# Half-size expert slots without TensorE's prefetch hint for the next slot's branch

## The chip, the cores and the metric

The kernel runs on one core of one Trainium2 chip. The metric is device microseconds for one execution. A core has five engines with an instruction stream each: PE (TensorE, whose weight loads the profile lists apart as PEld), DVE, ACT, POOL and SP. PEq (or PEldq), DVEq and so on stand for an engine's sequencer, which issues its instructions, branches and semaphore instructions. SP issues nearly all of the DMAs here.

## What is computed

Three stages follow one another: attention with a learned position bias, a gated dense layer, and a layer of eight experts in which each of 1152 tokens goes to one expert. The change lies in the last one:

```python
def _moe2_ref(x, w_gate, w1, w2, capacity):
    logits = x @ w_gate                       # x: 1152 x 512, 8 experts
    expert_idx = np.argmax(logits, axis=1)
    ...                                       # softmax; gate_w is the chosen expert's share
    for i in range(N):                        # capacity = 288 tokens for an expert
        e = expert_idx[i]
        if counts[e] < capacity:
            disp[e, counts[e]] = x[i]
            ...
    h = np.maximum(np.einsum('ecd,edf->ecf', disp, w1), 0.0)   # 512 -> 1024
    y = np.einsum('ecf,efd->ecd', h, w2)                       # 1024 -> 512
    for i in range(N):
        if keep[i]:
            out[i] = gate_w[i] * y[expert_idx[i], pos[i]]
```

## The kernel before

**Slots.** How many tokens an expert gets is known on the chip alone. The kernel sorts the experts by their count and works through nine slots, `e` = 0 to 8, the fullest first. Slots 0 and 1 always run the code for a full expert (`full`). For the others there are four ladders of code, one behind the other, each with a body for every slot that it may be needed for: `full` from line 1404, `mid1` and `mid2` (65 to 128 tokens) from line 1410, `few1` and `few2` with `q` = 2 (half-size slots, up to 64 tokens) from line 1418, and the same two with `q` = 4 (quarter-size, up to 32 tokens) from line 1428. The counts sit in registers (`ns`), and nested `If`s choose: the outer one leaves a ladder when the slot is too small for it, and the inner one skips a body that an earlier ladder has already done.

**How a ladder is left.** In the half-size ladder the outer `If` of slot `e` has the label `q{e}` (line 1420, whose branches the profile gives as L1418), and the inner one the label `d{e}` (L1421). When slot `e + 1` has too few tokens, each engine takes the branch of `q{e + 1}`, goes to a small arm behind the last body of the ladder, waits there until its own semaphores have caught up with what the skipped bodies would have counted (an EVENT_SEMAPHORE row), and goes on to the next ladder. SP's arms have one such row for each of eight DMA semaphores.

**Hints.** `hint(label, ...)` (line 1081) puts one BRANCH_PREFETCH_HINT instruction, in a block of its own, into TensorE's stream (and into others that it names): the branch with that label is likely to be taken. The hints that stand ahead of the loops' branches are `big` in the last fixed slot (line 1316), `b{e + 1}` in `mid1` (line 1205), both for TensorE, DVE and ACT, and `q{e + 1}` in the half-size bodies (line 1423), for TensorE alone. The quarter-size ladder has none.

**A half-size body.** `few1` multiplies 64 rows of tokens with the expert's first matrix (`ps_sh`, L1152, 16 products of the program, 32 MATMUL rows in the trace), DVE makes `hst` from it, TensorE transposes it (L1168); `few2` transposes the next slot's rows (L1078), spreads the gate (L1019), multiplies with the second matrix (`ps_sy`, L1196), and `finish` scales on DVE (L1040) and scatters to the output from POOL (L678). A quarter-size body is the same with 32 rows. `load_next` (line 726) has SP load the weights of slot `e + 3` and the rows of slot `e + 6`.

**Places in the stream.** `align(n)` at a ladder's end (lines 1409, 1417, 1427) puts the code behind it at a fixed offset in 256 instructions. All of this lies in a manual schedule: the instructions stand in the order in which the code is written.

Of the kernel before, what the change touches and what calls it, by code (L numbers as in the profile page):

```python
# [514 lines left out]
def moe_kernel(ctx, tc, shape, qd, kd, vd, wb, geo, wg, wv, wo, g2, e1, e2, ebase, desc, tri, out, cap):  # L515
# [13 lines left out]
    NS = NE + 1  # L529
# [179 lines left out]
    def load_e(e):  # L709
        for n in range(8):  # L710
            k = e % 3
            if (k, n) not in raws:
                raws[k, n] = (raw_tile if k == 0 else praw if k == 2 and n < 4 else eraw(k))(F32)
            src = e1 if n < 4 else e2
            i = nc.sync.dma_start(raws[k, n], src[bass.ds(ids[e], 1), n % 4].rearrange("o p n -> (o p) n"))
            fetched.setdefault((k, n), []).append((e, i.ins))
# [9 lines left out]
    def load_next(e, more=True):  # L726
        if e + 3 < NS:
            with tc.If(nio[e + 3] > 0):  # L728
                load_e(e + 3)
                if more:  # L730
                    with tc.If(nio[e + 3] > P):
                        load_xr(e + 3, nc.gpsimd)
        if e < NS - 6:
            load_xd(e + 6)
# [49 lines left out]
    with ExitStack() as pools:  # L784
# [35 lines left out]
        def route_a(tg, parts=1):  # L820
            yt = tp.tile([P, DM], F32, tag="dt", name="yt")
            for h in range(parts):
                ps = rtile("ps_yt")
                for kc in range(h * KC // parts, (h + 1) * KC // parts):
                    nc.tensor.transpose(ps[:, kc * P:(kc + 1) * P], y[:, tg, kc * P:(kc + 1) * P], ident)
                c = slice(h * DM // parts, (h + 1) * DM // parts)
                nc.scalar.copy(yt[:, c], ps[:, c])
            rt[tg] = yt

        def route_b(tg):  # L830
            yt = rt.pop(tg)
            ps = rtile("ps_lt")
            for kc in range(KC):
                nc.tensor.matmul(
                    ps[kc * GC:(kc + 1) * GC, :P], g2_sb[:, kc], yt[:, kc * P:(kc + 1) * P],
                    start=True, stop=True, skip_group_check=True,
                )
            lt = tp.tile([P, P], F32, tag="sg", name="lt")
            nc.scalar.copy(lt, ps[:, :P])
            rt[tg] = lt  # L840

        def route_l(tg):
            lt = rt.pop(tg)
            lg = rtile("ps_r")[:, :NE]
            nc.tensor.matmul(lg, lt, sel, start=True, stop=True)
            sc = tp.tile([P, 4, NE], F32, tag="rsc", name="rsc")
            s1 = tp.tile([P, 4], F32, tag="rs1", name="rs1")
            mx, m2, nmx = (s1[:, i:i + 1] for i in range(3))
            oh = ohs[:, tg]
            nc.vector.reduce_max(mx, lg, axis=mybir.AxisListType.X)  # L850
            nc.vector.scalar_tensor_tensor(sc[:, 1], lg, mx, desc_sb, ALU.is_ge, ALU.mult)
            nc.vector.reduce_max(m2, sc[:, 1], axis=mybir.AxisListType.X)
            nc.vector.tensor_scalar(oh, desc_sb, m2, None, ALU.is_equal)
            nc.vector.tensor_scalar_mul(nmx, mx, -1.0)
            nc.vector.tensor_tensor(cum[:, tg + 1], cum[:, tg], oh, ALU.add)
            dot(sc[:, 3], ebase_sb, oh, reb[:, tg:tg + 1])
            rt[tg] = lg, nmx, sc

        def route_gate(tg):
            lg, nmx, sc = rt.pop(tg)  # L860
            nc.scalar.activation(sc[:, 2], lg, AF.Exp, bias=nmx, accum_out=rsm[:, tg:tg + 1])
# [6 lines left out]
        def route_pos(t0, t1):  # L868
            n = (t1 - t0) * NE
            pos = rtile("ps_p")[:, :n]  # L870
            nc.tensor.matmul(
                pos, tri_sb[:, :P], ohs[:, t0:t1].rearrange("p t e -> p (t e)"), start=True, stop=False
            )
            nc.tensor.matmul(pos, ones, cum[:, t0:t1].rearrange("p t e -> p (t e)"), start=False, stop=True)
            rt[t0, t1] = pos

        def route_c(t0, t1):
            pos = rt.pop((t0, t1))
            r = slice(t0, t1)
            for tg in range(t0, t1):  # L880
                sc = tp.tile([P, 4, NE], F32, tag="rsc", name="rsc")
                dot(sc[:, 0], pos[:, (tg - t0) * NE:(tg - t0 + 1) * NE], ohs[:, tg], rps[:, tg:tg + 1])
            nc.vector.tensor_scalar(rsl[:, r], rps[:, r], float(cap), BIG, ALU.is_ge, ALU.mult)
            nc.vector.tensor_scalar_add(rsm[:, r], rsm[:, r], 1e-9)
            if t1 - t0 == 1:
                nc.vector.scalar_tensor_tensor(rsi[:, r], rps[:, r], reb[:, r], rsl[:, r], ALU.add, ALU.add)
            else:
                nc.vector.tensor_tensor(rps[:, r], rps[:, r], reb[:, r], ALU.add)
                nc.vector.tensor_tensor(rsi[:, r], rps[:, r], rsl[:, r], ALU.add)
            nc.vector.reciprocal(y[:, r, DM:DM + 1], rsm[:, r].unsqueeze(2))  # L890
            for tg in range(t0, t1):
                scatter(disp[:, :], rsi[:, tg:tg + 1], y[:, tg, :], disp_w)
# [173 lines left out]
    def load_xr(e, q):  # L1066
        read_rows(q.dma_start(xr[e][:, 0, :], rows(e, P, P)))
        read_rows(q.dma_start(xr[e][:cr - P, 1, :], rows(e, 2 * P, cr - P)))
# [12 lines left out]
    def hint(label, *more):  # L1081
        with tc.block():
            tc.mark_branch_hint_location(label, hint="LikelyTaken", engines=[mybir.EngineType.PE, *more])

    def align(n):
        for eng, a in ((e, a) for e, a in ALIGN.items() if n < len(a)):
            getattr(nc, eng).addr_align(a[0], offset=a[n], max_nops=0)
# [10 lines left out]
    def wsplit(e, n):  # L1098
        for i in split(*pair(e, n), weights(e)[n].rearrange("p a n -> p (a n)")):
            own(i, e, n)  # L1100
# [281 lines left out]
    with tc.manual_schedule():  # L1382
        full(0, {
            0: [
                lambda: route_pos(T - 2, T - 1), lambda: route_c(T - 2, T - 1), lambda: route_a(T),
                lambda: route_l(T - 1), lambda: route_gate(T - 1), lambda: wsplit(0, 1),
            ],
            1: [
                lambda: route_b(T), lambda: route_pos(T - 1, T), lambda: route_c(T - 1, T),
                lambda: wsplit(0, 4),  # L1390
            ],
            2: [lambda: route_l(T), lambda: route_gate(T)],
            (2, "y"): [lambda: route_pos(T, TG), lambda: route_c(T, TG), order_experts],
            4: [begin],
        })
        load_e(2)
        with tc.If(nio[2] > P):
            load_xr(2, nc.gpsimd)
        load_next(0)
        guessed = len(out_w)  # L1400
        full(1)
        load_next(1)
        del out_w[:guessed]
        with ExitStack() as nest:
            for e in range(FIX, NS):
                nest.enter_context(tc.If(ns[e] > P, label="big" if e == FIX else f"f{e}"))
                full(e)
                load_next(e)
            align(2)
        with ExitStack() as nest:  # L1410
            for e in range(FIX, NS):
                nest.enter_context(tc.If(ns[e] > M1, label=f"b{e}"))
                with tc.If(ns[e] <= P, label=f"m{e}"):
                    mid1(e)
                    mid2(e)
                    load_next(e, False)
            align(3)
        with ExitStack() as nest:  # L1418
            for e in range(FIX, NS):
                nest.enter_context(tc.If(ns[e] > (M1 // 2 if e >= QUADS else 0), label=f"q{e}"))  # L1420
                with tc.If(ns[e] <= M1, label=f"d{e}"):  # L1421
                    if e < NS - 1:
                        hint(f"q{e + 1}")
                    few1(e, 2)
                    few2(e, 2)
                    load_next(e, False)
            align(4)
        with ExitStack() as nest:
            for e in range(QUADS, NS):
                nest.enter_context(tc.If(ns[e] > 0, label=f"z{e}"))  # L1430
                with tc.If(ns[e] <= M1 // 2, label=f"s{e}"):
                    few1(e, 4)
                    few2(e, 4)
                    load_next(e, False)
# [82 lines left out]
```

## Time and profile before

| | |
|---|---|
| runs | 508.31, 511.47, 510.93 us, median 510.93 |
| profiled execution | 511.36 us |
| its span, first to last instruction | 509.7 us |
| PE busy | 490.2 us (96%) |
| DVE, ACT, POOL busy | 370.1, 265.5, 102.1 us |
| last mid-size body on PE ends | 478.5 us from the span's start |
| half-size body on PE | 480.07 to 489.81 us |
| two quarter-size bodies on PE | 492.31 to 504.3 us |

In this execution one slot runs as mid-size, one as half-size and two as quarter-size, so the change meets one executed body. The rows ahead of the prediction are whole lines of the views. A row of an operation gives how often it ran and its shortest, median and longest time in ns; a wait names the engine that waited, for whom, and the idle microseconds, times and longest.

### The profile page before, as it was taken

To read this page: it belongs to the slowest core of one execution; us is meant where nothing else is said; L and a number is where in the kernel's file an instruction comes from. 1 tells how busy PE (TensorE), PEld (TensorE's weight loads), DVE (VectorE), ACT (ScalarE), POOL (GpSimd) and SP (SyncE) were. 2 spreads that over 40 slices of the span, in tenths; PEclk is the share of its full clock that TensorE was granted. 3 is DMA by queue.
4 is the path that set the end of the run, shared out by engine and by line. 5 is a ranking of instruction groups with operands and counts; after the bars stand their busy time and mean duration, and the time that the engine had idled before them with its cause. 6 is when DMAs were issued, how large, how long until landed. Compare 5 with 4: busy or idle time off the path is not lost. (4 is left out here: it accounts for less than half of the span.)

```text
span 509.7 us, 11908 instructions
## 1 busy us (share of the span) xinstructions
PE 490.2 (96%) x4357; PEld 405.5 (80%) x4357; DVE 370.1 (73%) x924; ACT 265.5 (52%) x604; POOL 102.1 (20%) x218
## 2 busy tenths in 40 slices
PE   7999999999999999999999999999999899999875
PEld 3467777677778999978999889999877678897554
DVE  6899999998997899996799827633356683546321
ACT  5798899998876545453544203422222534437210
POOL 1054444445551100000000000000011231702213
PEclk9999999999999999999999999999999989999989
DMA  7799789999312944353231000000013985899640
GB/s 266 262 340 336 257 272 308 314 373 290 95 50 69 323 140 139 115 182 118 80 120 50 1 1 0 2 0 1 0 43 88 395 312 167 296 407 348 234 188 11
DMA packets 50084, 89.11 MB, mean 175 GB/s; under 512 B 7970, under 2 KB 27428, under 8 KB 50000
## 3 DMA queue, kind: packets, MB, share of 16 engines
q1 hardware_dynamic: 48560, 85.04, 49.1%
q0 software_dynamic: 1296, 3.03, 1.6%
q8 instruction: 40, 0.66, 0.5%
q14 instruction: 44, 0.36, 0.2%
q10 hardware_dynamic: 144, 0.02, 0.0%
HBM read 67.00 MB, written 22.15 MB: 175 GB/s over the span
## 5 line engine op out<-in xcount | busy, mean ns | idle before, releaser
L594 PE MATMUL ps_gv<-xh,hl 128*128 128x384 f32 x528 | 135.0, 336 | 0.0
L594 PEld LDWEIGHTS ps_gv<-xh,hl 128*128 128x128 f32 x528 | 95.3, 188 | 0.1
L594 PE MATMUL ps_gv<-xl,hl 128*128 128x384 f32 x264 | 88.7, 336 | 0.0
L902 PE MATMUL ps_o<-hl,hh 128*128 128x512 f32 x216 | 73.3, 404 | 0.3 <-ACT y L907 0.3
L117 DVE TENSOR_SCALAR bt<-geo_sb 128x320 f32<-128x320 f32 (+17 forms) x144 | 58.6, 458 | 0.0
L222 ACT ACTIVATE e_sb<-e_sb,mn 128x576 f32<-128x576 f32 x72 | 56.3, 783 | 1.5 <-DVE mn L214 1.3
L235 POOL TENSOR_SCALAR e_sb<-e_sb,rs 128x576 f32<-128x576 f32 x72 | 53.3, 752 | 18.2 <-DVE rs L231 15.8
L678 POOL DMA_INDIRECT disp<-y,rsi x9 | 9.7, 1079 | 233.8 <-DVE rs L850 205.2
L214 DVE CUSTOM_DVE_ANT_0 e_sb<-ps_s,bias_sb 128x576 f32<-128x576 f32 x72 | 51.6, 751 | 2.2 <-DMA bias_sb<-bias_d 1.2
L594 PEld LDWEIGHTS ps_gv<-xl,hl 128*128 128x128 f32 x264 | 49.6, 188 | 0.1
L902 PEld LDWEIGHTS ps_o<-hl,hh 128*128 128x128 f32 x216 | 40.5, 188 | 10.5 <-issue 1.4
L300 PE MATMUL ps_x<-et,vn 128*64 128x128 f32 (+1 forms) x800 | 47.5, 267 | 0.9 <-DVE xl L318 0.8
L197 PE MATMUL ps_s<-kst,qst 64*128 64x288 f32 (+1 forms) x320 | 45.6, 423 | 0.0
L604 ACT CAST hh<-sg 128x384 fp32r<-128x384 f32 x36 | 18.4, 512 | 48.1 <-DVE sg L603 48.1
L300 PEld LDWEIGHTS ps_x<-et,vn 128*64 128x64 f32 x800 | 39.3, 137 | 4.1 <-DVE xl L318 1.5
L902 PE MATMUL ps_o<-hl,hlo 128*128 128x512 f32 x105 | 42.1, 401 | 0.0
L577 ACT CAST hl<-dg 128x512 fp32r<-128x512 f32 x32 | 19.1, 621 | 39.4 <-PE ps_o L902 21.6
L197 PEld LDWEIGHTS ps_s<-kst,qst 64*128 64x128 f32 (+1 forms) x320 | 27.0, 178 | 5.0 <-DVE mn L214 0.8
L264 PEld LDWEIGHTS ps_t<-ident,e_sb 64*128 64x128 f32 x576 | 25.2, 139 | 5.1 <-issue 0.9
L603 DVE TENSOR_TENSOR sg<-ps_gv,sg 128x384 f32<-128x384 f32 x35 | 19.3, 553 | 12.6 <-PE ps_gv L594 12.6
L1275 PE MATMUL ps_h<-dxh,hl 128*128 128x288 f32 x128 | 26.9, 301 | 0.9 <-DVE hl L565 0.9
L602 DVE TENSOR_TENSOR sg<-ps_gv,sg 128x384 f32<-128x384 f32 x35 | 19.3, 552 | 10.8 <-ACT sg L601 10.4
(237 smaller groups left out, 910.4 us busy)
## 6 DMA issues: line engine op xcount, KB each, us to landing
eraw<-e SPq DMA_DIRECT2D x24, 512.0 KB, 9.5
bias_d<-bo SPq DMA_DIRECT2D x36, 295.5 KB, 4.3
raw<-e SPq DMA_DIRECT2D x16, 512.0 KB, 10.2
raw<-wo SPq DMA_DIRECT2D x12, 512.0 KB, 4.4
raw<-wg SPq DMA_DIRECT2D x11, 512.0 KB, 3.8
raw<-wv SPq DMA_DIRECT2D x11, 512.0 KB, 5.0
disp<-zero SPq DMA_DIRECT2D x9, 520.0 KB, 4.7
bias_sb<-bias_d SPq DMA_DIRECT2D x16, 288.0 KB, 3.8
```

The lines of the kernel that those rows point to most:

```text
L117: nc.vector.tensor_scalar(t[:, :m], dist_sb[:, :m], nbp[:, r:r + 1], None, ALU.max)
L197: nc.tensor.matmul(pss[j][i, half, :HS], qst[c * B + bb][d, p, i], kst[d, bb * NP + p, half * HS:(half + 1) * HS], start=True, stop=True, ...
L214: nc.vector.tensor_tensor_reduce(out=e[:, j, :].rearrange("p (a n) -> p a n", a=2), in0=ps[:, :, :HS], in1=bias_sb[c, p][:, j, :].rearrang ...
L222: nc.scalar.activation(e[:, j, :], e[:, j, :], AF.Exp, bias=mn[:, j:j + 1], scale=-1.0, accum_out=sm[:, j:j + 1])
L235: nc.gpsimd.tensor_scalar(e[:, j, :], e[:, j, :], rs, 1.0, ALU.mult, ALU.mult)
L264: nc.tensor.transpose(tp_t[u, h][:, n * HP:(n + 1) * HP], e[r, n * P:(n + 1) * P], ident[r, r])
L300: nc.tensor.matmul(ps[j * D:(j + 1) * D, o:o + n], vn[:, p, bb, jc, j * D:(j + 1) * D], et[:, t0:t0 + n], start=jc == NF, stop=jc == NF - ...
L594: nc.tensor.matmul(ps[:, :TN], w_[:, n, kc, :], x_[:, kc, t * TN:(t + 1) * TN], start=i == 0, stop=i == 3 * KC - 1,)
L602: nc.vector.tensor_tensor(sg, pss[0][:, :TN], sg, ALU.mult)
L603: nc.vector.tensor_tensor(sg, pss[1][:, :TN], sg, ALU.mult)
L902: nc.tensor.matmul(ps, ht_cols(f, a, tg), wot[f][b_], start=i == 0, stop=i == len(ops) - 1)
L1275: nc.tensor.matmul(ps[:, :CAP], part(e, f // 2, a)[:, kc, f % 2 * P:(f % 2 + 1) * P], x_[:, kc], start=i == 0, stop=i == 3 * KC - 1,)
```

## The change

One call is left out: in a half-size body TensorE is no longer told that the branch of the next slot is likely to be taken. The hints `big` and `b{e + 1}` stay.

```diff
                 with tc.If(ns[e] <= M1, label=f"d{e}"):
-                    if e < NS - 1:
-                        hint(f"q{e + 1}")
                     few1(e, 2)
                     few2(e, 2)
                     load_next(e, False)
```

On TensorE, at the head of slot 3's half-size body (the one that runs here), the order changes as follows; `raw` holds the weights, `xt` the transposed rows.

```order
 L1418 COMPARE_AND_BRANCH
 L1421 COMPARE_AND_BRANCH
-L1082 UNCONDITIONAL_BRANCH
-L1513 BRANCH_PREFETCH_HINT
-L1082 UNCONDITIONAL_BRANCH
 L1152 MATMUL ps_sh<-raw_5234,xt_5640 64x256
 L1152 MATMUL ps_sh<-raw_5238,xt_5640 64x256
```

The hint and the two branches of its block go, and the products follow the slot's two comparisons directly. It is the same in each of six bodies (slots 2 to 7). At the end of this body nothing moves: the program's branch around the arm of line 728 and the next comparison, L1418, stay as they are.

```order
L1196 MATMUL ps_sy<-raw_5248,sht 64x256 x2
L728 UNCONDITIONAL_BRANCH
L1421 UNCONDITIONAL_BRANCH
L1418 COMPARE_AND_BRANCH
L1421 COMPARE_AND_BRANCH
L1082 UNCONDITIONAL_BRANCH
L1513 BRANCH_PREFETCH_HINT
```

These are the rows before the change, from the last products of slot 3 to the head of slot 4; the first L1418 row among them is the branch `q4`, the one that the removed hint was for. On the other engines only the block's branches go, as on DVE at a half-size body's head:

```order
 L1418 COMPARE_AND_BRANCH
 L1421 COMPARE_AND_BRANCH
-L1082 UNCONDITIONAL_BRANCH x2
 L1164 TENSOR_SCALAR hst<-ps_sh 128x256 x2
 L1173 COPY sht<-ps_st 128x256 x2
```

Every other instruction of the program, with its waits, is the same and in the same place.

## Rows read from the trace of the kernel before

**Rows 1.** The page, parts 1 and 3: engines, and the two instruction queues.
```profile
PE 490.2 (96%) x4357; PEld 405.5 (80%) x4357; DVE 370.1 (73%) x924; ACT 265.5 (52%) x604; POOL 102.1 (20%) x218
q8 instruction: 40, 0.66, 0.5%
q14 instruction: 44, 0.36, 0.2%
```
**Rows 2.** The chain that ended last, in order of time: start, us, what.
```profile
492.03 0.28 issue
492.31 2.50 PE ps_sh L1152 x32
...
502.32 2.00 PE ps_sy L1196 x64
...
504.40 0.36 DVE ob L1040
...
505.53 1.07 POOL out_dram L678
```
**Rows 3.** Timeline of PE, 470 to 511: start, us, operation [idle before <-releaser].
```profile
478.11 0.40 PE L1240 MATMUL ps_my<-hl,mhh 128*128 128x512 f32 x1
480.07 2.34 PE L1152 MATMUL ps_sh<-raw,xt 128*64 128x256 f32 x18 [1.56 <-ACTq L1421]
482.57 1.94 PE L1152 MATMUL ps_sh<-raw,xt 128*64 128x256 f32 x14 [0.16 <-issue]
...
486.14 3.67 PE L1196 MATMUL ps_sy<-raw,sht 128*64 128x256 f32 x32
492.31 2.50 PE L1152 MATMUL ps_sh<-eraw,xt 128*32 128x256 f32 x32 [2.50 <-SPq L1410]
```
**Rows 4.** Line 1513, the hints that ran: engine, count, ns, first and last start.
```profile
L1513 PEldq BRANCH_PREFETCH_HINT  x3: 36/40/41, 444.2 to 479.8; - x3
```
**Rows 5.** Line 1418, 487 to 491.5: TensorE's branch out of the half-size ladder.
```profile
L1418 PEldq COMPARE_BRANCH  x1: 3551/3551/3551, 487.8 to 487.8; - x1
L1418 PEldq EVENT_SEMAPHORE  x1: 51/51/51, 491.4 to 491.4; - x1
```
**Rows 6.** Line 1404, 462 to 464: TensorE's branch hinted as `big`.
```profile
L1404 PEldq COMPARE_BRANCH  x1: 388/388/388, 462.9 to 462.9; - x1
```
**Rows 7.** Line 1410, 476 to 478.6: TensorE's branch hinted as `b3`.
```profile
L1410 PEldq COMPARE_BRANCH  x1: 349/349/349, 476.7 to 476.7; - x1
```
**Rows 8.** Line 1428, 503 to 507: TensorE's branch without a hint.
```profile
L1428 PEldq COMPARE_BRANCH  x1: 3284/3284/3284, 503.7 to 503.7; - x1
```
**Rows 9.** DMA queues, 480 to 481.2: packets, MB, share of 16 engines.
```profile
q8 instruction: 1, 0.02, 5.0%
```
**Rows 10.** DMA queues, 481.3 to 488.8: every queue that moved anything.
```profile
DMA packets 831, 2.90 MB, mean 386 GB/s; under 512 B 118, under 2 KB 118, under 8 KB 828
q1 hardware_dynamic: 748, 2.71, 94.1%
q0 software_dynamic: 80, 0.16, 5.7%
q14 instruction: 3, 0.02, 1.0%
```
**Rows 11.** DMA queues, 488.8 to 490.
```profile
q8 instruction: 1, 0.02, 5.7%
```
**Rows 12.** Waits of PE, and SP's own, 478 to 493: us, times, longest.
```profile
PE ps_sh L1152 <- SPq L1410: 2.5, 1, 2.5
PE ps_sh L1152 <- ACTq L1421: 1.6, 1, 1.6
SPq L1410 <- SPq L1410: 9.8, 1, 9.8
```
**Rows 13.** Line 1410, 481 to 492.2: SP's arm that catches up, eight semaphores.
```profile
L1410 SPq EVENT_SEMAPHORE  x8: 17/17/17, 491.6 to 492.1; - x8
```
**Rows 14.** Weight loads of PE, waits, 478 to 493.
```profile
PEld ps_sh L1152 <- issue: 3.5, 2, 2.9
```

## The prediction

> **What bounds the kernel now.** I read the page first. PE is busy for 490.2 of 509.7 us [rows 1], so whatever PE waits for is nearly always time at the end. But the change touches PE in six bodies of which few run, so the share matters less than one place: the end of the half-size body and the step into the quarter-size ladder. Three views lead there.
>
> The chain that ended last begins at 492.03 us [rows 2]. From there PE's two quarter-size bodies run to 504.3, DVE scales the last result, POOL scatters it at 505.53, and the output's write and the closing barrier end the span. So a microsecond more or less at PE's start of 492.31 is a microsecond at the end, unless something else would hold PE back.
>
> The timeline of PE shows one half-size body: its 32 `ps_sh` rows stand at 480.07 (18) and 482.57 (14), and its last products end at 486.14 + 3.67 = 489.81 [rows 3]. Then PE idles for 2.50 us, until 492.31. This is the only idle stretch that the removed hint could concern: the profile has three hints on TensorE, and the last, at 479.8, is the one that goes [rows 4].
>
> What ends that idle time? Two things, and they end together. First, TensorE's branch at L1418, the one that the hint was for, took 3551 ns from 487.8, and its catch-up row follows at 491.4 [rows 5]. Second, the wait itself is put down to SP at L1410: SP waited 9.8 us there [rows 12], and its eight catch-up rows come only at 491.6 to 492.1 [rows 13]. The chain starts at 492.03, inside those eight, and not at the branch's end.
>
> **What the change removes, and what each piece costs.**
>
> *The hint instruction.* One of the removed hints runs in this execution, 36 ns on the sequencer [rows 4]. It stands ahead of the body's first product, but there PE idles 1.56 us until ACT's catch-up at L1421 [rows 3, 12], so those 36 ns are hidden. Without that cover they would be worth 0.04 us. The block's branches at L1082 have no row in the trace at all, on any engine, so I cost them at nothing. Five of the six removed hints lie in bodies that do not run.
>
> *What the hint buys.* Here is the heart of it. Two other hinted branches of TensorE out of a ladder took 388 and 349 ns [rows 6, 7]. One without a hint took 3284 ns [rows 8]. The branch under change has a hint and took 3551 [rows 5]: it stands with the unhinted one, not with the hinted two. A second view says the same. Queue q8 carries 40 instruction packets in 0.66 MB, about 16 KB each [rows 1]. One lands between 480 and 481.2, just after the hint [rows 9]. None at all moves between 481.3 and 488.8, while the body runs [rows 10]. The next comes between 488.8 and 490, after the branch has already begun at 487.8 [rows 11]. If the hint had brought the target in, the branch would not have had to wait for that packet. The packet at 480 must be the code of the body itself: the products stop after 18 of 32 rows and go on at 482.57 with "issue" as the reason [rows 3], as they would where the stream runs into a piece that has just come. So in this execution the hint was issued and its target was not there when it was wanted. I take its worth as zero, and the branch after the change as between 3284 and 3551 ns: 0 to 0.27 us less.
>
> The Trainium skill, "Runtime: NRT & Kernel Launch", section "Instruction fetch mechanics", says that instructions come in blocks of 16 KiB and that a taken branch whose target is outside the window must fetch it before execution goes on. The packets of 16 KB and the 3284 ns agree with that. The rule speaks against the change: by it alone a branch that loses its hint falls from a hit to a fetch, and the sum would be some 3 us longer. The row of 3551 ns is what it has to be weighed against: the fetch is paid already.
>
> *What a shorter or longer branch is worth.* Even a branch that hit would gain little. From the branch's end to the first product PE now needs 492.31 − (487.78 + 3.55) = 0.98 us. With a hit of about 0.37 us (mean of 388 and 349) PE would be ready at 487.78 + 0.37 + 0.98 = 489.13, or at 489.81 when its own products end. SP's catch-up, at 491.6 to 492.1, would then hold it to about 492.1. So here the hint's full worth is at most 492.31 − 492.03 = 0.28 us, and the 0.27 us of the last paragraph can give back no more. I take 0.1, between 0 and 0.27.
>
> *The code behind.* Each body is one instruction shorter on TensorE, so the place where the products stop after 18 rows may move by one instruction. What the stop costs is 0.16 us on PE [rows 3]; it can be 0 or that. The 3.5 us that the weight loads spend on "issue" [rows 14] are the same stop and the branch, seen from the other side of PE, and are not added. The quarter-size ladder is put at its fixed offset again by the alignment at line 1427, so nothing moves there.
>
> **Sum.** The profiled execution took 511.36 us, 509.7 of span and 1.66 around it. 511.36 + 0 (hint, hidden) − 0.1 (branch) + 0 (stop) = 511.3. Its own bounds are −0.43 (0.27 and 0.16) and +0.1. The profiled execution lies 0.43 above the median of the three runs, 510.93, and so the same sum on the median gives 510.8. The runs themselves lie between 508.31 and 511.47, 3.2 us apart, far wider than any term here; the likeliest case's own range is therefore 508.2 to 511.6.
>
> **Rivals.**
>
> *The hint usually works, and the profiled execution is the exception: slower.* The place is the same branch, L1418 at 487.8. Its price is 3.55 − 0.37 = 3.18 us if nothing else holds PE. That the three runs are 3.2 us apart, about the price of one such branch, speaks for it; so do the 388 and 349 ns of the other two hinted branches. Against it speaks that SP's catch-up at 491.6 would hold PE anyway. It decides from the point where SP is done before PE would be, that is when SP's loads land over 2 us earlier (by 489.8, the end of PE's products). Then the removal costs up to 492.31 − 489.81 = 2.5 us, or 3.18 if the products end earlier too: 513.4 to 514.1. While SP is as late as here it costs at most 0.28: 511.2. The rule of the Trainium skill named above would come out here: a lost hint is a fetch in the path.
>
> *The hint is in the way: faster.* No packet of q8 moves in the 7.5 us after the one at 480 [rows 10]. If an unserved hint blocks the ordinary fetching ahead, or delays the packet for which the products stop, its removal could save the stop and the excess of this branch over the unhinted one: 0.16 + 0.27 = 0.43 us, 510.5 on the median. SP's catch-up caps the sum at 0.28.
>
> *The change does nothing that runs.* Of the bodies that the edit touches only one runs here, but that one does lose its hint row; were it none, the time would be the 510.9 of before, which lies in the main case anyway.
>
> **How the numbers follow.** The main case gets 0.80, the slower rival 0.11, the faster one 0.06, and 0.03 is left for a shift that I don't see. About 1%, 5.1 us, is what a measurement of this kernel can tell from no change. The slower rival's worst, 514.1, is 0.6% up, and the faster rival's best is 0.1% down, so neither passes that bound without help from the scatter of the runs. Hence 0.02 faster, 0.95 within 1%, 0.03 slower. The predicted time is the main case's, 510.8. The range begins at that case's lower end, 508.2, and reaches past its upper end to 512.6, part of the way into the slower rival, since the main case alone holds little over 0.7 of the chance within its own range.
>
> **What the profile of the changed kernel would show.** The last hint of TensorE stands near 464, two rows in all. The branch at the half-size body's end (still L1418) takes 3.2 to 3.6 us. A packet of q8 between 483 and 487, which is missing now, would show that the lost hint had blocked the ordinary fetching; with none there, the hint was simply without effect. PE's first quarter-size product starts at 492 to 492.4, with SP's catch-up as its releaser. I would be wrong if SP's catch-up comes well before 491 and PE still starts at 492 or later: then the branch alone sets the end, and the hint's worth must be looked for in runs that have it. I would be wrong as well if the branch takes under 1 us without its hint, or well over 3.6.

## The result and the profile after

| | before | after |
|---|---|---|
| median | 509.81 us (21 runs, 508.25 to 512.58) | 512.62 us (21 runs, 510.94 to 514.82) |
| ratio, 95% interval | | 1.0052, 1.0035 to 1.0070 |
| profiled execution, its span | 511.36, 509.7 us | 511.31, 509.5 us |

The removed hint costs 0.52%, 2.65 us of 509.81 (1.8 to 3.6 by the interval). The predicted time was 510.8 us; the measured one lies just outside the range, 0.02 above its end of 512.6, and within the 1% that was called no change.

The two profiled executions took the same time, and that is chance: before's lies 1.55 us above its kernel's median, after's 1.31 below its own. One place where they differ by chance lies 60 us ahead of the change: in before the clock fell from 415 us on, in after it did not. These are the windows of both, before first (stretch, us, then busy us and count of PE, PEld, DVE, ACT and POOL, the granted clock, the DMA share, GB/s):

```profile
415.00:418.00 3.00, 3.00 (x11) 2.52 (x11) 1.88 (x7) 1.92 (x3) 0.79 (x1) 0.51 0.76 295
```
```profile
415.00:418.00 3.00, 3.00 (x20) 2.73 (x19) 2.27 (x6) 2.27 (x3) 0.64 (x1) 1.00 0.73 283
```

So the two are compared from the half-size body on. Its branch first, on TensorE (count, shortest, median and longest ns, first and last start):

```profile
L1418 PEldq COMPARE_BRANCH  x1: 5272/5272/5272, 485.4 to 485.4; - x1
```

With the hint it took 3551 ns [rows 5]; without it takes 5272, which is also 1988 ns more than the branch that never had a hint [rows 8]. The timeline of PE after the change (start, us, operation, idle before and its releaser):

```profile
478.37 3.81 PE L1152 MATMUL ps_sh<-raw,xt 128*64 128x256 f32 x32 [1.54 <-ACTq L1421]
482.12 0.44 PE L1168 MATMUL ps_st<-ident,hst 128*128 128x128 f32 x2
...
483.82 3.67 PE L1196 MATMUL ps_sy<-raw,sht 128*64 128x256 f32 x32
491.69 3.54 PE L1152 MATMUL ps_sh<-eraw,xt 128*32 128x256 f32 x32 [4.19 <-PEq L1418]
...
498.63 2.08 PE L1152 MATMUL ps_sh<-praw,xt 128*32 128x256 f32 x32
```

Two rows of the timeline before that belong beside these:

```profile
484.44 0.44 PE L1168 MATMUL ps_st<-ident,hst 128*128 128x128 f32 x2
...
498.82 2.05 PE L1152 MATMUL ps_sh<-praw,xt 128*32 128x256 f32 x32
```

Against [rows 3]: the stop after 18 rows of `ps_sh` is gone, and the half-size body takes 483.82 + 3.67 − 478.37 = 9.12 us where it took 9.74. All 0.62 us of it lie in the first products: from the first of them to the first L1168 row it is 4.37 us before and 3.75 after. Then PE idles 4.19 us instead of 2.50, and its releaser is its own sequencer at the branch, not SP. SP's arm, which ended the wait in [rows 13], is still running when PE starts at 491.69, so it holds nothing:

```profile
L1410 SPq EVENT_SEMAPHORE  x8: 17/17/17, 491.3 to 491.8; - x8
```

The 32 products after the pause take 3.54 us instead of 2.50. From the end of the half-size body to the first product of the second quarter-size body it is 498.63 − 487.49 = 11.14 us, where before has 498.82 − 489.81 = 9.01: 2.13 longer, 1.69 of it idle time; the other 0.44 goes with the clock. Less the 0.62 of the stop, it is 1.51 us longer from the half-size body's first product on: this pair of profiles shows less than the 2.65 of the medians. After (columns as above):

```profile
491.60:495.20 3.60, 3.51 (x33) 1.86 (x33) 0.00 (x0) 0.00 (x0) 0.00 (x0) 0.53 0.01 2
495.20:496.60 1.40, 1.39 (x10) 0.90 (x8) 0.69 (x3) 0.58 (x1) 0.00 (x0) 0.98 0.02 6
```
And before, at the same work:
```profile
492.30:494.80 2.50, 2.48 (x33) 1.28 (x33) 0.00 (x0) 0.00 (x0) 0.00 (x0) 0.75 0.16 50
494.80:496.70 1.90, 1.90 (x10) 1.57 (x8) 0.80 (x3) 0.58 (x1) 0.00 (x0) 0.50 0.01 4
```

A clock of 0.50 is the level of 1.2 GHz, 1.00 that of 2.4. After the longer pause nearly the whole first product stage ran at the low level (0.53); before paid part of it there (0.75) and part in the transposes behind. So of the 1.04 us more in `ps_sh` only 0.44 stays at the body's end.

What the branch waited for stands with the instruction queue. The page counts 41 packets of q8, one more than before [rows 1]:

```profile
q8 instruction: 41, 0.67, 0.5%
```

The DMA queues of after from 479.5 us to the branch, then from the branch to 490 us (packets, MB, share of 16 engines):

```profile
q1 hardware_dynamic: 559, 2.05, 92.0%
q0 software_dynamic: 80, 0.16, 7.1%
q14 instruction: 4, 0.03, 1.6%
```
```profile
q1 hardware_dynamic: 363, 1.04, 61.1%
q8 instruction: 2, 0.03, 3.4%
q14 instruction: 3, 0.02, 2.3%
```

From 479.5 us to the branch there is no packet of q8, as in [rows 10], and then there are two instead of the one of [rows 11]: they begin at 486.6 and 487.6 in the trace, one behind the other, and the branch ends 1.5 us after the second has landed. So it waited for two pieces of 16 KB. Which piece of code a packet carries the profile does not say; that is read from counts and times here and in what follows.

### The profile page after: what moved, and what is told of

Same layout as the page of the kernel before. It is cut to its first block, busy times and chain, and to the rows that moved or that the text cites. A ratio compares the mean times of both kernels' runs of the same rounds, so it can differ in the third digit from the quotient of the medians.

```text
span 509.5 us, 11907 instructions
## 1 busy us (share of the span) xinstructions
PE 488.6 (96%) x4357; PEld 403.7 (79%) x4357; DVE 370.3 (73%) x924; ACT 265.3 (52%) x604; POOL 101.8 (20%) x218
```

## The experiments

Every comparison is with the kernel before on the same chip. In the quoted texts A is the account by which the packet ahead of the branch comes late and the hint is served only then; B, that SP's arm holds PE whatever the branch does; C, that without the hint a useless next piece is fetched first and the branch pays for two. The letters that follow in the later texts carry these further; each text says what it expects by them. Of each kernel there is one profile, and executions of one kernel lie up to 7 us apart (g1), so verdicts on time rest on the ratios and the profile says only what happened in that execution.

**The place of the body in its pieces of code.** The half-size ladder starts 22 instructions earlier in its piece, so that the body steps into the next one 22 later.

```diff
-    ALIGN = {"tensor": (256, 240, 131, 40, 0), "vector": (128, 85, 10), "scalar": (128, 89, 100, 0, 0)}
+    ALIGN = {"tensor": (256, 240, 131, 18, 0), "vector": (128, 85, 10), "scalar": (128, 89, 100, 0, 0)}
```

> The kernel before with its hint, but the half-size ladder's code placed 22 instructions earlier in its 256 (tensor offset 18 instead of 40), so that the body steps into the next 16 KB piece later, after some 29 of its 32 first products instead of 18. Theory A (late packet): before, the body reached the next piece just as its packet came, and then nothing was fetched ahead until the branch; given more time, the step finds the piece there, a q8 packet moves about 1 us after the step, and the hinted branch at L1418 takes under 0.5 us instead of 3.55. PE idles under 1 us ahead of the first quarter-size product instead of 2.5, and the time is 2.5 to 3.5 us shorter than before (0.5 to 0.7%). Theory B (the prediction's: SP's catch-up holds PE until about 492 anyway): the branch may become short, but PE still starts as late, and the time is at most 0.3 us shorter (0.06%).

Ratio 1.0002 (0.9985 to 1.0020). Branch, and PE's first quarter-size products:

```profile
L1418 PEldq COMPARE_BRANCH  x1: 2616/2616/2616, 488.3 to 488.3; - x1
```
```profile
491.88 1.93 PE L1152 MATMUL ps_sh<-eraw,xt 128*32 128x256 f32 x32 [1.55 <-SPq L1421]
```

The body stops once, after 29 rows, for 0.45 us. The packet begins at 488.47, 0.19 us after the branch. The branch of [rows 8], which fetches for itself, has its packet 0.98 us behind its start (504.67 and 503.69); in the other 13 profiles that last branch has it 0.98 to 1.53 us behind. So this one had been asked for earlier: I read it as the hint's, and late. A expected a branch under 0.5 us and 0.5 to 0.7% less time; neither came. In this profile SP's arm at L1410 was done by 490.3 us:

```profile
L1410 SPq EVENT_SEMAPHORE  x8: 17/17/17, 489.8 to 490.3; - x8
```

PE started at 491.88 all the same, 0.98 us behind the end of its own branch, so here it was the branch that held it: B's unchanged time came, but not for B's reason.

The same place without the hint:

```diff
-    ALIGN = {"tensor": (256, 240, 131, 40, 0), "vector": (128, 85, 10), "scalar": (128, 89, 100, 0, 0)}
+    ALIGN = {"tensor": (256, 240, 131, 18, 0), "vector": (128, 85, 10), "scalar": (128, 89, 100, 0, 0)}
...
-                    if e < NS - 1:
-                        hint(f"q{e + 1}")
```

> The changed kernel (no hint) with the same earlier place. Theory A: the step into the next piece finds it there, the piece behind that is fetched during the body, and at the branch one packet alone is left to fetch: 3.2 to 3.6 us as in before, PE idle about 2.5 us, time within 0.15% of before, and 2.5 to 3 us shorter than the changed kernel. A rival, C (a branch without a hint always fetches two packets in a row): 5.3 us as in the changed kernel, 0.4 to 0.6% longer than before.

Ratio 1.0057 (1.0035 to 1.0079): 513.54 against 510.31 for the same place with the hint. Branch, and the queue from 487 to 491 us:

```profile
L1418 PEldq COMPARE_BRANCH  x1: 5274/5274/5274, 486.6 to 486.6; - x1
```
```profile
q8 instruction: 2, 0.03, 4.6%
```

Two packets and 5.27 us again, as in after, where A expected one and 3.2 to 3.6 us. The place is not the cause; the hint is, and C's two packets show.

**When the hint is given.** It is moved from the body's head to the middle of its first products, inside `few1`.

```diff
+                if q == 2 and s == 1 and kc == 1 and e < NS - 1:
+                    hint(f"q{e + 1}")
...
-                    if e < NS - 1:
-                        hint(f"q{e + 1}")
```

> The hint moved from the head of the half-size body to the middle of its first products, behind the step into the next piece; place as before (offset 40). Theory A: what is pending is served at a step or at the branch, and no step follows; the branch takes 3.5 us with one packet, time as before within 0.15%. A rival, D (a hint starts its own fetch when the queue is idle; in before it came while the queue was busy and was put off): a q8 packet about 1 us after the hint, near 484, the branch under 0.5 us, 2.5 to 3.5 us shorter than before (0.5 to 0.7%).

Ratio 1.0008 (0.9990 to 1.0026). Branch, and PE:

```profile
L1420 PEldq COMPARE_BRANCH  x1: 1336/1336/1336, 489.8 to 489.8; - x1
```
```profile
480.69 2.34 PE L1154 MATMUL ps_sh<-raw,xt 128*64 128x256 f32 x18 [1.53 <-ACTq L1423]
484.67 1.89 PE L1154 MATMUL ps_sh<-raw,xt 128*64 128x256 f32 x14 [1.64 <-issue]
...
492.96 1.93 PE L1154 MATMUL ps_sh<-eraw,xt 128*32 128x256 f32 x32 [1.10 <-DVEq L1420]
```

The packet comes at 488.32: 3.6 us after the hint at 484.7 and 1.5 us ahead of the branch. It has landed before the branch begins (489.7), but a branch that waits ends 1.2 to 1.6 us after its packet's landing in these profiles (2.4 in e2), and this one takes 1.34 us. That is neither A's 3.5 nor D's under 0.5. A hint's packet is real, and it takes microseconds to come. What the branch wins, the body loses in the stop of 1.64 us.

**Any hint, or the right one?** The hint stays, but names the quarter-size ladder's branch, which is not the next to be taken.

```diff
-                        hint(f"q{e + 1}")
+                        hint(f"z{max(e + 1, QUADS)}")
```

> The hint stays at the head of the half-size body but names the branch out of the quarter-size ladder (z4), which is not taken there and whose target lies in another piece. Theory A (what is pending is fetched first when the branch is reached): two packets at the branch, the wrong target and then the right one, 5.0 to 5.5 us, 0.4 to 0.6% longer than before, as without the hint. A rival, E (any hint at this place only stops the ordinary fetching ahead, and its target plays no part): one packet, 3.5 us, time as before within 0.15%.

Ratio 1.0057 (1.0038 to 1.0077), as without a hint. Branch, and the queue from 489 to 493 us:

```profile
L1418 PEldq COMPARE_BRANCH  x1: 4945/4945/4945, 488.6 to 488.6; - x1
```
```profile
q8 instruction: 2, 0.03, 5.0%
```

So the instruction as such does nothing; its target does. With a wrong target there are two packets, as without a hint, so one of them is of no use to the branch; E's single packet did not come.

**The loads taken away.** While the mid-size and half-size bodies run, SP's queue moves the 4 MB of slot 5. Here, in the next kernel and in g3 they are left out behind slot 2's body, so slot 5's output is made with other weights; the rest of the work is the same.

```diff
-    def load_next(e, more=True):
-        if e + 3 < NS:
+    def load_next(e, more=True, own_weights=True):
+        if e + 3 < NS and own_weights:
...
                     mid2(e)
-                    load_next(e, False)
+                    load_next(e, False, e != FIX)
```

> The kernel before, with its hint, but the 4 MB of weights for slot 5 are not loaded behind the mid-size body (left out; slot 5 then uses slot 2's weights), so that the DMA queues are nearly idle while the half-size body runs. Theory F (instruction packets wait in the DMA queues behind the weight loads: each was asked for in time, at the step into a new piece, and came 3 to 6 us late): q8 packets come 1.0 to 1.4 us after the step, the body runs without the gap after 18 rows, the hinted branch at L1418 takes 0.3 to 0.5 us, PE idles 1.0 to 1.3 us ahead of the first quarter-size product, and the time is 2.5 to 4 us shorter than before (0.5 to 0.8%). Theory G (the lateness belongs to this step or this hint and not to the loads): branch 2.5 to 3.6 us as before, time within 0.2% of before. Theory B (SP's catch-up holds PE) can't be told apart here, since SP's arm has less to wait for as well.

Ratio 0.9968 (0.9946 to 0.9990), 508.96 us. Branch, PE, and the queues from 480.5 to 485.8:

```profile
L1418 PEldq COMPARE_BRANCH  x1: 351/351/351, 485.9 to 485.9; - x1
```
```profile
489.03 1.93 PE L1152 MATMUL ps_sh<-eraw,xt 128*32 128x256 f32 x32 [1.10 <-DVEq L1418]
```
```profile
q0 software_dynamic: 80, 0.16, 8.2%
q8 instruction: 1, 0.02, 1.1%
q14 instruction: 2, 0.02, 0.9%
q1 hardware_dynamic: 1, 0.00, 0.0%
```

With the queues nearly empty, the hint's packet comes in the body, at 481.2 us, and the branch is a hit like those of [rows 6, 7]. F has the mechanism; the gain of 0.32% is under its 0.5 to 0.8%.

The same without the hint:

```diff
-                    load_next(e, False)
+                    load_next(e, False, e != FIX)
...
-                    if e < NS - 1:
-                        hint(f"q{e + 1}")
```

> The same without slot 5's weights, and without the hint. Theory F: the piece behind is fetched 1.0 to 1.4 us after the step, long before the branch; at the branch one packet is left, 3.2 to 3.5 us as the unhinted branch at the end has; PE idles 4.0 to 4.3 us, counted as in the run with the hint plus 3 us; time 3 to 4 us above the run with the hint (0.6 to 0.8%) and within 0.2% of before. Theory G: 5.3 us and two packets at the branch, 0.4 to 0.6% above before.

Ratio 1.0015 (0.9994 to 1.0036), 510.84 us: 1.88 more than with the hint. Branch, and the queue from 487 to 490.8:

```profile
L1418 PEldq COMPARE_BRANCH  x1: 3749/3749/3749, 487.0 to 487.0; - x1
```
```profile
q8 instruction: 1, 0.02, 2.2%
```

One packet comes in the body (481.9), and one behind the branch's start (487.9). So, read by these times, the useless piece is fetched without the loads too; only it is there in time, and the branch pays for its own alone. The hint is worth 0.37% here, where F expected 0.6 to 0.8%. That is C as far as the number of packets goes, and it says what the loads do: they move the first packet from the body to the branch.

**The loads split.** Half of a slot's weights are loaded one body later. In the first of the two the hint stays.

```diff
-    def load_e(e):
-        for n in range(8):
+    def load_e(e, parts=range(8)):
+        for n in parts:
...
     def load_next(e, more=True):
+        if e > FIX and e + 2 < NS:
+            with tc.If(nio[e + 2] > 0):
+                load_e(e + 2, range(4, 8))
         if e + 3 < NS:
             with tc.If(nio[e + 3] > 0):
-                load_e(e + 3)
+                load_e(e + 3, range(4 if e >= FIX else 8))
```

> A full kernel with the hint: from slot 2 on, SP loads a later slot's first matrix behind one body and its second matrix behind the next body, so that behind the mid-size body 2 MB are queued instead of 4. Theory F: the queues are empty by about 481 to 482, when the half-size body steps into the next piece; its packet comes 1.0 to 2 us after the step, the branch takes under 1 us, PE idles under 1.6 us, time 2 to 3.5 us below before (0.4 to 0.7%). The first quarter-size body must not wait for slot 5's second matrix (needed near 500). Theory G: no change in the branch, time within 0.2% of before.

Ratio 0.9989 (0.9966 to 1.0012). Branch, and the queues from 482 to 484:

```profile
L1421 PEldq COMPARE_BRANCH  x1: 2676/2676/2676, 486.1 to 486.1; - x1
```
```profile
q14 instruction: 1, 0.01, 1.8%
```

I had not expected this: for 2 us nothing but one small packet moves, and TensorE's piece still does not come (486.49, 0.34 us behind the branch, so by e1's reading asked for before it). F expected a branch under 1 us. The loads are a cause, by f1, but a plain queue behind them is not the whole of it.

The same split without the hint:

```diff
                 with tc.If(ns[e] <= M1, label=f"d{e}"):
-                    if e < NS - 1:
-                        hint(f"q{e + 1}")
```

> The same split loads without the hint. Theory F: the piece behind is fetched in time and one packet is left at the branch, 3.3 us, or up to 4.5 if the second half of the loads is then in the queues; 2.5 to 3.5 us above the split kernel with the hint (0.5 to 0.7%), near before. Theory G: two packets, 5.3 us, 0.4 to 0.6% above before.

Ratio 1.0081 (1.0053 to 1.0110), 514.64 against 510.17 us: the largest worth of a hint here, 4.47 us. Branch, and PE:

```profile
L1421 PEldq COMPARE_BRANCH  x1: 6044/6044/6044, 487.6 to 487.6; - x1
```
```profile
494.64 3.64 PE L1155 MATMUL ps_sh<-eraw,xt 128*32 128x256 f32 x32 [4.95 <-PEq L1421]
```

Two packets come, at 487.3 and 491.1 us: F's single one did not, and the branch took longer than G's 5.3 us.

**Place again.** If the place decides whether the piece is there when the hint is served, an offset moved the other way or together with the loads must show it. The split loads with the hint, at offset 18:

```diff
-    ALIGN = {"tensor": (256, 240, 131, 40, 0), "vector": (128, 85, 10), "scalar": (128, 89, 100, 0, 0)}
+    ALIGN = {"tensor": (256, 240, 131, 18, 0), "vector": (128, 85, 10), "scalar": (128, 89, 100, 0, 0)}
...
+                load_e(e + 2, range(4, 8))
...
-                load_e(e + 3)
+                load_e(e + 3, range(4 if e >= FIX else 8))
```

> A full kernel with the hint, the split loads of the run before and TensorE's half-size ladder placed at 18 instead of 40. Theory H (both conditions are needed: a step into a new piece asks for what comes next only if that piece is already there, and under loads a piece comes 2 to 4 us after it was asked for): with half the loads the body's next piece is there 1.5 us into the body, the step comes 2.4 us into it, the hint's target follows 1 to 1.5 us after the step, the branch at L1418 takes 0.3 to 0.5 us, PE idles 1.0 to 1.3 us, time 0.4 to 0.7% below before. Theory F (only the queues' load matters): the branch as in the split run, 2.7 us, or shorter if the queues are empty then.

Ratio 0.9960 (0.9930 to 0.9989), faster than before. Branch, and PE:

```profile
L1421 PEldq COMPARE_BRANCH  x1: 956/956/956, 489.6 to 489.6; - x1
```
```profile
492.60 1.93 PE L1155 MATMUL ps_sh<-eraw,xt 128*32 128x256 f32 x32 [0.98 <-DVEq L1421]
```

The packet comes at 488.1, 1.4 us ahead of the branch. The full loads at offset 5, with the hint:

```diff
-    ALIGN = {"tensor": (256, 240, 131, 40, 0), "vector": (128, 85, 10), "scalar": (128, 89, 100, 0, 0)}
+    ALIGN = {"tensor": (256, 240, 131, 5, 0), "vector": (128, 85, 10), "scalar": (128, 89, 100, 0, 0)}
```

> The kernel before with its hint and the half-size ladder placed at 5 instead of 40, all loads as before: the step comes some 35 instructions later, about 4 us into the body. Theory H: the next piece is there by then, the step asks for the hint's target at once, its packet comes 1.5 to 4 us after the step (485 to 487.5 on the scale of before), the branch takes 0.4 to 2.5 us, PE idles 1.1 to 2 us, time 0.1 to 0.5% below before. Theory F: the packet waits for the loads to end, 488 to 489, branch 2.5 to 3.6 us, time as before.

Ratio 0.9986 (0.9957 to 1.0016).

```profile
L1418 PEldq COMPARE_BRANCH  x1: 3236/3236/3236, 489.2 to 489.2; - x1
```

The packet is as late as ever (490.0), although the body ran without a stop: H falls. And without slot 5's loads, with the step moved earlier:

```diff
-    ALIGN = {"tensor": (256, 240, 131, 40, 0), "vector": (128, 85, 10), "scalar": (128, 89, 100, 0, 0)}
+    ALIGN = {"tensor": (256, 240, 131, 76, 0), "vector": (128, 85, 10), "scalar": (128, 89, 100, 0, 0)}
...
-                    load_next(e, False)
+                    load_next(e, False, e != FIX)
```

> Slot 5's weights left out as in the earlier pair, with the hint, but TensorE's half-size ladder placed at 76 instead of 40, so that the body steps into the next piece with its very first products, before that piece can be there. The queues are empty. Theory H: the step comes too early, what the hint names isn't asked for there, and its packet comes some 4 to 6 us later or at the branch; branch 1 to 3.5 us, time 1 to 3 us above the run without these loads at 40 (0.2 to 0.6%). Theory F: with empty queues the packet comes 1.0 to 1.4 us after the step and the branch takes 0.35 us; time as that run's.

Ratio 0.9959 (0.9927 to 0.9991).

```profile
L1418 PEldq COMPARE_BRANCH  x1: 351/351/351, 486.2 to 486.2; - x1
```

A hit (packet at 480.8), although the step came so early that the body began with 1.91 us of idle time. With the loads away the hint is in time at either place; with them, late at three (40, 18 and 5).

**A version that uses it.** From slot 2 on, a slot's weights are loaded two slots ahead instead of three; SP then issues slot 5's loads from 485.0 us on instead of 475.7, inside the half-size body.

```diff
-        if e + 3 < NS:
+        if e > FIX and e + 2 < NS:
+            with tc.If(nio[e + 2] > 0):
+                load_e(e + 2)
+        if e + 3 < NS and (e < FIX or more):
             with tc.If(nio[e + 3] > 0):
-                load_e(e + 3)
+                if e < FIX:
+                    load_e(e + 3)
```

> A full kernel with the hint at its old place (40): from slot 2 on, SP loads a slot's weights two slots ahead instead of three, so slot 5's 4 MB are issued behind slot 3's choice, near 482, and not behind the mid-size body. Theory F (the loads are what makes TensorE's instruction packets late): U's next piece and the hint's target come within 2.2 us of their steps, before or as the loads begin; the branch at L1418 takes 0.35 to 1 us, PE idles 1.0 to 1.3 us, no stretch at the half clock follows, time 0.3 to 0.6% below before, as in the run without these loads. Slot 5's first matrix must be there at about 494; if the loads land later than that, the second quarter-size body waits instead and the gain is lost. Theory G' (it is the amount in the queues at any time while the body runs, not at the steps): branch 2.5 to 3.5 us, time as before.

Ratio 0.9977 (0.9961 to 0.9992), 508.87 us: faster than both kernels, though the 0.23% below before is less than the 0.3 to 0.6% expected. The hint's packet comes at 482.1, ahead of the loads. Branch, PE, and the queues from 481.5 to 484:

```profile
L1422 PEldq COMPARE_BRANCH  x1: 351/351/351, 487.3 to 487.3; - x1
```
```profile
490.42 1.93 PE L1156 MATMUL ps_sh<-eraw,xt 128*32 128x256 f32 x32 [1.12 <-DVEq L1422]
```
```profile
q8 instruction: 1, 0.02, 3.1%
```

**All of them at one place.** The stretch from the half-size body's first product to the second quarter-size body's first, in the one profile of each, beside the ratio of its median:

| kernel | hint | branch, ns | PE idle, then `ps_sh`, us | stretch, us | ratio |
|---|---|---|---|---|---|
| g1 split loads, offset 18 | yes | 956 | 0.98, 1.93 | 15.33 | 0.9960 |
| g3 loads left out, offset 76 | yes | 351 | 1.10, 1.93 | 15.44 | 0.9959 |
| f1 loads left out | yes | 351 | 1.10, 1.93 | 15.50 | 0.9968 |
| h1 loads later | yes | 351 | 1.12, 1.93 | 15.51 | 0.9977 |
| f3 split loads | yes | 2676 | 1.62, 1.93 | 16.00 | 0.9989 |
| e1 offset 18 | yes | 2616 | 1.55, 1.93 | 16.74 | 1.0002 |
| e3 hint later | yes | 1336 | 1.10, 1.93 | 17.63 | 1.0008 |
| g2 offset 5 | yes | 3236 | 2.18, 3.16 | 17.86 | 0.9986 |
| f2 loads left out | no | 3749 | 2.66, 2.51 | 18.11 | 1.0015 |
| before | yes | 3551 | 2.50, 2.50 | 18.75 | 1 |
| e4 wrong target | wrong | 4945 | 3.90, 3.37 | 19.71 | 1.0057 |
| after | no | 5272 | 4.19, 3.54 | 20.26 | 1.0052 |
| e2 offset 18 | no | 5274 | 4.19, 3.64 | 20.71 | 1.0057 |
| f4 split loads | no | 6044 | 4.95, 3.64 | 23.02 | 1.0081 |

The ratios rise with the stretch, so this is where the differences come from. Two rows stand out, g2 and before itself: before's 18.75 us lies by f2's 18.11 (1.0015), while its ratio of 1 belongs by e1's 16.74 (1.0002). Both profiled executions were long ones, 3.09 and 1.55 us above their kernels' medians. In g2 the half-size body begins at 482.31 us, later than in all the others but g1 (482.63), so much of its excess lies ahead of this stretch; in before it begins at 480.07, in the middle of the fourteen. I read from it that in before's the hint's packet came later than it mostly does; there is only one trace of before, so this is argued, not shown.

## Why the prediction was wrong

**The hint's own cost, and where it acts: right.** Two hints are left, one half-size body runs, and the half-size body loses no time at its head: PE idles 1.54 us there, as it did 1.56 [rows 3], until ACT's catch-up. The other engines' busy times are within 0.3 us of before's.

**"I take its worth as zero": the step that failed.** The prediction compared 3551 ns with a hint [rows 5] to 3284 without one at another branch [rows 8], and concluded that the hinted branch had already paid the whole fetch. The price of the branch without its hint at this place was never in the trace of before, and it is not 3284 but 5272 ns (5274 in e2, 4945 with a wrong target). All nine kernels with the right hint count 40 packets of q8 on their pages, all four without it 41, the one with a wrong target 42. The account that fits these counts: without the hint the sequencer asks for the next piece in line, which the branch jumps over, and under the weight loads that piece is as late as the hint's was; the branch waits for it and then for its own. With the hint it waits for one. So a late hint is still worth a packet. That the piece in line is asked for agrees with what the Trainium skill, "Runtime: NRT & Kernel Launch", section "Instruction fetch mechanics", says: that prefetch is purely sequential, and that a taken branch out of the window fetches its target first. The kernels with the right hint show what that rule does not speak of: by the counts and times of packets (f1 and f2 above all), the hint puts the branch's target in place of the useless piece.

The packet at 488.8 [rows 11] was read as the branch's own, since it began after the branch had. By its time alone (1.07 us behind the branch's start) it may be that; but in e1 and f3 the one packet begins 0.19 and 0.34 us behind it, and in e3 and g1 1.5 and 1.4 us ahead. Those had been asked for before the branch, and came late. Which it was in before's profile stays open; the count of packets does not depend on it.

**"SP's catch-up caps any worth at 0.28 us": wrong.** SP's time of 491.6 to 492.1 was taken as given. In after SP's arm and PE's product overlap (491.3 to 491.8, 491.69), so when the branch got longer, PE fell behind SP at once. For a longer branch SP is no cap at all. Nor did it hold PE in before: in all nine kernels whose branch took over 2.6 us PE's first quarter-size product starts 0.91 to 1.00 us behind the branch's end, 0.98 in before, while SP's arm at the mid-size ladder ended anywhere from 11.6 us ahead of that product (f4) to 0.1 behind it (after). The prediction had this 0.98 in its hands and put the wait down to the SP row that stood next to it. Whether so late an arm would hold an earlier PE no run shows; in e1, with the same loads, it was done by 490.3. What a hit leaves was mis-sized too: PE does not start where the body's products end (489.81) but 1.10 to 1.12 us behind that place (f1, g3, h1).

**The sum had no term for the clock.** The longer pause lowers the granted clock for the products behind it: +1.04 us in `ps_sh`, 0.44 of it net in this pair.

**The stop after 18 rows: mis-sized.** It went in after, as the lower end had it, but that gave back 0.62 us and not 0.16: the idle time in [rows 3] is counted from the end of a row that lasts 0.38 us, while in the running stream a row starts every 0.11 us. In e3 and f4 the same kind of stop shows 1.64 and 1.62 us of idle time.

**The slower rival** had the right side: its price of 3.18 us stands near the measured 2.65, and near what the right hint saves at the other places (medians: e2 over e1 3.23, f2 over f1 1.88, f4 over f3 4.47). That nearness is luck: its mechanism, a hint that usually hits, is seen only where the loads are out of the way (f1, g3, h1: 351 ns), and in this pair the loss is a second packet and the clock. Its condition, SP done early, was not needed. **The faster rival** has its sign, a packet of q8 in 483 to 487 us, by the number alone (486.6): after's branch began 2.35 us sooner than before's, and the packet came 1.1 us behind it. Where the freed fetch is seen clearly (f2, 481.9), it brings a piece that the branch does not need, and the time rises.

**What the prediction named as its refutation** came: a branch well over 3.6 us in after, and, in f4, SP's arm done long before 491 (483.1) with PE's start at 494.64, set by the branch alone.

**Still open:** why TensorE's packet stays away for microseconds after the loads have left the queues nearly empty (in f3 from 481 to 484 us; it came at 486.5, when the next loads were moving), and why 22 instructions more ahead of the step bring it in time there (g1). That the loads delay it is shown by f1, f2, g3 and h1; how, is not.

## What to carry to other kernels

A hint whose branch is still slow is not a hint without effect: ask what the sequencer would fetch in its place, and take the price without it from the same place, by one run, before writing zero. Where code pieces travel beside large loads, look at the instruction queue's packets against the step into the next piece and the branch; issuing the loads behind the hint's packet (0.23% here) gave a hit of 351 ns. And read a worth of a few microseconds from several executions, not from one profile: before's lay 1.55 us from its own median.

## What the runs showed of the hardware

A packet of 16 KB of code takes about 1 us once it moves (0.9 to 1.4 us in most rows), but where slot 5's weights were loaded ahead (386 GB/s on the queues in [rows 10], half the data in f3, f4 and g1) the next one began 7.3 to 8.8 us after the half-size body's first product (5.5 in g1), and without them 1.5 to 2.3 us after it (f1, f2, g3, h1). The Trainium skill's page "Runtime: NRT & Kernel Launch", section "Instruction fetch mechanics", calls the crossing into the next piece mostly hidden; here PE stood idle for 0 to 1.64 us at the crossing, and for up to 4.95 us at the branch behind it.

A pause costs more than its length. In seven kernels PE idled 0.98 to 1.62 us ahead of the quarter-size products, and these took 1.93 us at a clock of 1.00, as in f1:

```profile
489.00:491.00 2.00, 1.97 (x33) 1.23 (x34) 0.00 (x0) 0.00 (x0) 1.08 (x1) 1.00 0.08 25
```

In the other seven it idled 2.18 to 4.95 us, and the same 32 rows took 2.50 to 3.64 us with the clock down to 0.50: up to 1.7 us on top of the idle time.
